# A third place for half of each group in the gradients of w1 and w2, and one buffer fewer for an output row

## The chip, the core and the metric

The kernel runs on one core of one Trainium2 chip. The metric is the time of one execution on the device, in microseconds (us). The core has five engines with their own instruction queues: TensorE (PE, matrix products, with weight loads shown apart as PEld), VectorE (DVE), ScalarE (ACT), GpSimd (POOL) and SyncE (SP). In this kernel SP issues the loads and POOL the stores; each queue is worked off in order.

## The reference

A gated mix of a spectral filter (a two-dimensional FFT, a product with a complex filter, the inverse) and a dense layer with squared ReLU, with its gradients by all inputs but B_x. What matters here is the dense layer and the gradients of its two weights:

```python
def _B_ref(x, w1, b1, w2, b2):          # x: 1 x 2048 x 1024, w1: 1024 x 3584, w2: 3584 x 1024
    h = jnp.einsum("bsd,df->bsf", x, w1) + b1
    zero = jnp.zeros_like(h)
    r = jnp.where(h > zero, h, zero)
    h = r * r
    out = jnp.einsum("bsf,fd->bsd", h, w2) + b2
    return out
# ...
g = _sigmoid((x * gate_w).sum(-1, keepdims=True))
return g * a + (1 - g) * b              # a: the spectral part, b: the dense part
# reference(): this output, and its vjp with grad_out
```

With db = (1 - g) * grad_out and dh = (db w2^T) * 2 r, the gradients are h^T db for w2 (3584 x 1024) and x^T dh for w1 (1024 x 3584). Both sum over the 2048 rows.

## The kernel before

Three stages follow each other on PE: a first one computes h2 = r * r and dh and stores both, turned, in DRAM (`h2T_scr`, `dhT_scr`); the second, `mlp_grads`, computes the two weight gradients; the third computes the dense output. Pieces of the FFT path are woven between their matrix products. In the profile the second stage lies from about 465 to 846 us.

The second stage goes through 14 groups of 512 columns: 7 of h2 (gradient of w2), then 7 of dh (gradient of w1). A group is loaded with four transposing DMAs into one of two tiles, `even` and `odd`:

```python
jobs = [(h2T_scr, fg) for fg in range(FG)] + [(dhT_scr, fg) for fg in range(FG)]
KH, FH = NT // 2, FGW // 2              # 8 row tiles, 256 columns
grp = {
    n: later["odd" if n % 2 else "even"][:].rearrange("p (t f) -> p t f", t=NT) for n in range(len(jobs))
}

def fetch(n, *halves):                  # column halves 0 and 1 of group n, each in two row halves
    if n < len(jobs):
        scr, fg = jobs[n]
        v_ = scr[:].rearrange("c p s -> (c p) s")[fg * FGW : (fg + 1) * FGW, :]
        for i in halves:
            f_ = slice(i * FH, (i + 1) * FH)
            for k in range(2):
                in_ = v_[f_, k * KH * P : (k + 1) * KH * P]
                after(turned(grp[n][:, k * KH : (k + 1) * KH, f_], in_), later["blocks"])
    elif n == len(jobs) and 1 in halves:
        later["block"] = blocks(h2T_scr)(0)
```

Each product is made of 2 x 2 quarters by Strassen's scheme in Winograd's form: seven chains of products, p1 to p7, in place of eight, with sums of quarters made on DVE beforehand. `a11`, `a12` are the two row halves of the first column half of a group, `a21`, `a22` those of the second; the sum S1 = a21 + a22 is written in place of a21.

```python
def left(g, *which, tie=None):
    (a11, a12), (a21, a22) = quads(grp[g], FH)
    # ... S3 = a11 - a21, S1 = a21 + a22 (in place), S2 = S1 - a11, S4 = a12 - S2

class Block:                            # 128 rows of either column half; two blocks to a group
    def __init__(self, k):
        self.g, self.part = divmod(k, 2)
        self.lo = wb.tile([P, D], BF16, name="wlo", tag="wlo", bufs=3)[:]
        self.hi = wb.tile([P, D], BF16, name="whi", tag="whi", bufs=2)[:]
        self.operands()

    def add(self, t_, h, kept):         # DVE; its line is 924 in the profile
        return V(out=self.side(t_, h), in0=self.flat(self.V[:]), in1=self.flat(kept[:]), op=ALU.add)

    def p1(self):
        self.X = mps.tile([P, H], FP32, name="pX", tag="pX", bufs=2)
        self.chain(self.X, self.a11, self.b11, True)
        self.c1 = self.kept("c1", 2)    # ACT copies pX
    def p2(self):
        self.V = mps.tile([P, H], FP32, name="pV", tag="pV", bufs=2)
        self.chain(self.V, self.a12, self.b21, True)
        self.first = self.add(self.lo, 0, self.c1)      # first half of the low rows
    def p5(self):
        self.chain(self.V, self.S[1], self.T[1], True)  # begins pV anew
    # ... p6, p7 on pX; p4 completes and stores self.hi
    def p3(self):
        self.chain(self.V, self.S[4], self.b22, False)
        self.ended = self.add(self.lo, 1, self.u2)      # second half of the low rows
        self.store(self.lo, 0)                          # POOL stores 256 KB
```

The class `Turned`, for the gradient of w1, does the same with x as the left operand and the group as the right one (products on line 987, sums of a group on line 1035; for w2 lines 913 and 887).

The order of the work in the steady state, the same in both halves of the stage:

```python
for k in range(2, NB // 2):
    a = blk.pop(k - 1)
    g, second = divmod(k, 2)
    b = blk[k] = Block(k)
    b.p1()
    b.p2()
    if second:
        fetch(g + 2, 0)
    a.p4()
    if not second:
        fetch(g + 1, 1)
    b.p6()
    a.p3()
    if second and g + 1 < FG:
        left(g + 1, 3, 1, tie=a.ended)
    # ...
    b.p5()
    b.p7()
    # ... left(g, 4), or left(g + 1, 2)
```

(`yield`s, at which pieces of the FFT path are put in, are cut.) At the passage from the seventh to the eighth group two blocks b and c of the gradient of w1 begin together: b.p1, b.p2, a.p4, a.p3, c.p1, c.p2, sum X3 of x, b.p5, b.p6, c.p5, c.p6, sum X4, b.p7, c.p7, b.p4, b.p3.

Of the kernel before, what the change touches and what calls it, by code (L numbers as in the profile page):

```python
# [10 lines left out]
P = 128  # L11
BF16 = mybir.dt.bfloat16
# [128 lines left out]
def kernel(  # L141
# [27 lines left out]
    S, D = xf.shape  # L169
    F = B_w1.shape[1]  # L170
    g = Geo(S, D, F)
    S2, DC, FC = g.S2, g.DC, g.FC
    R1, R2 = g.R1, g.R2
    NT = S // P
    Q, H, LW, W1 = D // 4, D // 2, g.Df + 1, g.Df
    FGW, FG, FGC = g.FGW, g.FG, g.FGC
# [4 lines left out]
    turned = lambda out, in_: nc.sync.dma_start(out=out, in_=in_, transpose=True)  # L181
# [12 lines left out]
    def pool(name, side="left", space=SBUF, stack=None, bufs=1):  # L194
        stack = ExitStack() if stack is None else stack
        kw = {} if space == DRAM else dict(side=side, reuse_waits="tile")
        return stack.enter_context(tc.tile_pool(name=name, bufs=bufs, space=space, **kw)), stack

    pers, _ = pool("pers", stack=ctx)
    dram, _ = pool("dram", space=DRAM, stack=ctx)  # L200
# [13 lines left out]
    h2T_scr = dram.tile([FC, P, S], BF16, name="h2T_scr")  # L214
# [19 lines left out]
    def after(ins, earlier, wait=mybir.DependencyClass.Sync):  # L234

        if earlier is not None:
            info = mybir.DependencyInfo(wait, mybir.DependencyReason.DATA)
            tc.add_manual_dep(ins.ins, earlier.ins.name, info, reason="paced")
# [386 lines left out]
    later = {}  # L625
# [183 lines left out]
    def mlp_grads():  # L809
        wb, wbs = pool("m2")  # L810
# [6 lines left out]
        def more_of_x(n, last):  # L817
            for t in range(len(loaded), min(len(loaded) + n, NT)):
                after(ld(out=xr[:, t, :], in_=x_perm[t]), last)
                loaded.append(t)  # L820

        jobs = [(h2T_scr, fg) for fg in range(FG)] + [(dhT_scr, fg) for fg in range(FG)]
        KH, FH = NT // 2, FGW // 2
        grp = {
            n: later["odd" if n % 2 else "even"][:].rearrange("p (t f) -> p t f", t=NT) for n in range(len(jobs))
        }

        def fetch(n, *halves):
            if n < len(jobs):
# [3 lines that stand above are left out]
                    f_ = slice(i * FH, (i + 1) * FH)  # L833
                    for k in range(2):
                        in_ = v_[f_, k * KH * P : (k + 1) * KH * P]
                        after(turned(grp[n][:, k * KH : (k + 1) * KH, f_], in_), later["blocks"])
            elif n == len(jobs) and 1 in halves:
                later["block"] = blocks(h2T_scr)(0)

        fetch(0, 0, 1)  # L840

# [13 lines left out]
        quads = lambda t_, w_: [[t_[:, j * KH : (j + 1) * KH, i * w_ : (i + 1) * w_] for j in range(2)] for i in range(2)]  # L855
# [15 lines left out]
            yield  # L871

        def left(g, *which, tie=None):
            (a11, a12), (a21, a22) = quads(grp[g], FH)
            made = S_.setdefault(g, {})
            for n in which:
                if n == 1:
                    made[1] = fp16(a21)
                else:
                    made[n] = sb.tile([P, KH, FH], FP16, name=f"S{n}", tag=f"S{n}", bufs=2 if n == 3 else 1)[:]  # L880
                x, y, op = {
                    3: lambda: (a11, a21, ALU.subtract),
                    1: lambda: (a21, a22, ALU.add),
                    2: lambda: (made[1], a11, ALU.subtract),
                    4: lambda: (a12, made[2], ALU.subtract),
                }[n]()
                later["sum"] = V(out=made[n], in0=x, in1=y, op=op)  # L887
                after(later["sum"], tie, mybir.DependencyClass.NoSync)

        class Block:  # L890

            def __init__(self, k):
                self.g, self.part = divmod(k, 2)
                self.lo = wb.tile([P, D], BF16, name="wlo", tag="wlo", bufs=3)[:]
                self.hi = wb.tile([P, D], BF16, name="whi", tag="whi", bufs=2)[:]
                self.operands()

            def operands(self):
                (a11, a12), (_, a22) = quads(grp[self.g], FH)
                self.A = {"11": a11, "12": a12, "22": a22, **S_.setdefault(self.g, {})}  # L900
                self.S, self.T = S_[self.g], T_
                self.a11, self.a12, self.a22 = a11, a12, a22
                self.b11, self.b21, self.b22 = b11, b21, b22
# [57 lines left out]
        class Turned(Block):  # L961

            def operands(self):
                (self.a11, self.a12), (_, self.a22) = quads(xr, H)
                (self.b11, self.b21), (_, self.b22) = quads(grp[self.g], FH)
                self.S, self.T = X_, T_[self.g]

            flat = staticmethod(lambda ap: ap.rearrange("p (j f) -> p j f", j=2))
# [49 lines left out]
                X_["last"] = made  # L1018

        def sums_of_group(g, *which, tie=None):  # L1020
            (g11, g21), (g12, g22) = quads(grp[g], FH)
            made = T_.setdefault(g, {})
            for n in which:
                if n == 3:
                    made[3] = fp16(g12)
                else:
                    tag = {1: "S3", 2: "S2", 4: "S4"}[n]
                    made[n] = sb.tile([P, KH, FH], FP16, name=f"G{n}", tag=tag, bufs=2 if n == 1 else 1)[:]
                x, y = {
                    1: lambda: (g12, g11),  # L1030
                    2: lambda: (g22, made[1]),
                    3: lambda: (g22, g12),
                    4: lambda: (g21, made[2]),
                }[n]()
                after(V(out=made[n], in0=x, in1=y, op=ALU.subtract), tie, mybir.DependencyClass.NoSync)  # L1035
# [23 lines left out]
        yield each  # L1059
        blk[1].p5()  # L1060
        left(0, 4)
        fetch(2, 0)
        yield each
        blk[1].p6()
        next(sums)
# [11 lines left out]
# [5 lines that stand above are left out]
            yield each  # L1082
# [3 lines that stand above are left out]
            yield each  # L1086
            a.p4()
            if not second:
                fetch(g + 1, 1)
            yield each  # L1090
            b.p6()
            yield each
# [3 lines that stand above are left out]
            if k >= 4:  # L1096
                more_of_x(2, a.last)
            yield each
            b.p5()
            if k == NB // 2 - 2:  # L1100
                sums_of_x(1, tie=a.ended)
            if k == NB // 2 - 1:
                sums_of_x(2, tie=a.ended)
            yield each
            b.p7()
            if not second:
                left(g, 4, tie=b.added)
            elif g + 1 < FG:
                left(g + 1, 2, tie=b.added)
            else:  # L1110
                sums_of_group(FG, 1, 2, tie=b.added)
            yield each
# [11 lines left out]
        flat = db_p.tile([P, NT * D], BF16, name="w2L", tag="dbn")  # L1124
        later["w2L"] = flat[:, 0 : FC * H].rearrange("p (c e) -> p c e", e=H)
        later["spare"] = flat[:, FC * H :]
        fetch(FG + 1, 1)
        yield each
        c.p1()
        yield each  # L1130
# [24 lines left out]
        for k in range(NB // 2 + 2, NB):  # L1155
            g, second = divmod(k, 2)
            b = Turned(k)
            b.p1()
            yield each
# [3 lines that stand above are left out]
            yield each  # L1163
            a.p4()
            if not second:
                sums_of_group(g, 3, 4)
            yield each
            b.p6()
            yield each
            a.p3()  # L1170
            if not second:
                fetch(g + 1, 1)
            yield each
            b.p5()
            yield each
            b.p7()
            if second and g + 1 < len(jobs):
                sums_of_group(g + 1, 1, 2, tie=b.added)
            yield each
            n = k - NB // 2 - 2  # L1180
            if n < FC // 4:
                rows_of_w2(later["w2L"], 4 * n, 0, b.added)
            a = b
# [11 lines left out]
    def blocks(scr):  # L1195
        v_ = scr[:].rearrange("c p s -> p c s")

        def one(k, earlier=None):
            t_ = later["odd" if k % 2 else "even"][:, 0 : FC * BW].rearrange("p (c b) -> p c b", b=BW)
            for h in range(2):  # L1200
                c_ = slice(h * FC // 2, (h + 1) * FC // 2)
                after(ld(out=t_[:, c_, :], in_=v_[:, c_, k * BW : (k + 1) * BW]), earlier)
            return t_

        return one
# [460 lines left out]
    for k in range(NT // 4):  # L1666
        i = 4 * k
# [129 lines left out]
```

## Time and profile before

| what | value |
|---|---|
| time, median of 3 runs | 1215.94 us (1215.14 to 1216.46) |
| span of the profiled run | 1213.8 us |
| TensorE clock granted | 0.999 of full speed |
| DMA moved | 234.44 MB, 193 GB/s on average |
| transposing loads from `h2T_scr` and `dhT_scr` | 56, four to a group |
| stores of `wlo`, of `whi` | 28 of 256 KB each, on POOL's queue |

How to read it: "busy" is the time in which an engine works on an instruction; waiting, branching and issuing of DMAs are not counted. A wait is put down to what released it last. "To landing" is the time from the issue of a DMA to its completion. In a table of stretches each row gives start and end, length, busy time of PE, PEld, DVE, ACT and POOL with the count of instructions, the granted clock, the busy share of the DMA engines and GB/s. `even` and `odd` hold the groups, `pX` and `pV` are the accumulators, `wlo` and `whi` the low and high output rows of a block, `S` and `G` sums of a group's quarters, `X` sums of x. Matrix products are pipelined, and their ends in the trace are modelled.

### The profile page before, as it was taken

Reading aid. Unit: us, or ns where it says so; the run is one execution under the profiler, and the core shown is the slowest. Engines: PE = TensorE matmul, PEld = TensorE weight load, DVE = VectorE, ACT = ScalarE, POOL = GpSimd, SP = SyncE. Lnnn points to the kernel's source line nnn. Section 1 sums busy time; section 2 is a strip of 40 time slices with the busy share of each in tenths; the row PEclk is TensorE's granted clock in tenths of the full one; section 3 lists DMA queues with packets and bytes.
Section 4 is the critical chain, followed back from the end, with each engine's and each line's share of the span. In section 5 each row is a group of like instructions: output and inputs, shape, how many; then the busy total and the mean of one; then the engine's idle time right before and its main releaser. Section 6 shows DMA issues by size and latency. Waiting matters only on the chain. (4 is left out here: it accounts for less than half of the span.)

```text
span 1213.8 us, 20077 instructions
## 1 busy us (share of the span) xinstructions
PE 1189.0 (98%) x7229; PEld 653.8 (54%) x7328; DVE 827.5 (68%) x1808; ACT 620.7 (51%) x1128; POOL 361.0 (30%) x587
## 2 busy tenths in 40 slices
PE   9999999999999999999999999999999999999997
PEld 5555555544444444444447889888444444444443
DVE  3546466586788977887789556665389756966464
ACT  4658767736777773444445245554455422332322
POOL 0124424413455542333333434444131000000000
PEclk9999999999999999999999999999999999999999
DMA  9668566486758598998998799956875699965550
GB/s 278 214 173 191 165 170 215 132 168 194 203 178 209 178 242 138 213 221 201 238 207 163 163 250 216 212 170 180 269 217 173 193 212 221 247 198 174 160 148 35
DMA packets 332383, 234.44 MB, mean 193 GB/s; under 512 B 197773, under 2 KB 291115, under 8 KB 332283
## 3 DMA queue, kind: packets, MB, share of 16 engines
q1 hardware_dynamic: 301856, 142.50, 52.2%
q0 software_dynamic: 30224, 90.61, 24.0%
q8 instruction: 57, 0.93, 0.3%
q14 instruction: 44, 0.35, 0.1%
q10 hardware_dynamic: 202, 0.04, 0.0%
HBM read 107.24 MB, written 81.81 MB: 156 GB/s over the span
## 5 line engine op out<-in xcount | busy, mean ns | idle before, releaser
L725 PE MATMUL ph<-xT,w1g 128*128 128x512 bf16 x866 | 214.6, 379 | 3.0 <-DMA w1g<-in_B_w_dram 1.2
L733 PE MATMUL pd<-dbT,w2T 128*128 128x512 bf16 x874 | 210.0, 379 | 1.0
L733 PEld LDWEIGHTS <-w2T 128*128 128x128 bf16 x896 | 87.1, 98 | 101.8
L737 DVE SCALAR_TENSOR_TENSOR dhT<-pd,rT 128x512 bf16<-128x512 f32 x112 | 76.8, 686 | 87.9 <-PE pd L733 76.1
L725 PEld LDWEIGHTS <-w1g 128*128 128x128 bf16 x896 | 85.2, 98 | 93.3 <-DMA w1g<-in_B_w_dram 1.5
L726 ACT ACTIVATE rT<-ph,b1col 128x512 bf16<-128x512 f32 x112 | 77.3, 690 | 67.3 <-PE ph L725 60.4
L987 PEld LDWEIGHTS <-res 128*128 128x128 bf16 (+1 forms) x896 | 86.7, 98 | 12.2 <-issue 2.0
L1339 PEld LDWEIGHTS <-dS 128*128 128x128 f16 x574 | 55.9, 98 | 66.3
L226 POOL DMA_DIRECT2D z_scr<-u x96 | 58.6, 616 | 105.5 <-ACT u L294 51.0
L226 POOL DMA_DIRECT2D r<-y_scr x96 | 58.3, 612 | 104.7 <-issue 44.4
L419 ACT CAST x<-px 64x512 f16<-64x512 f32 x128 | 74.1, 579 | 18.0 <-PE px L416 16.9
L727 ACT ACTIVATE h2T<-rT 128x512 bf16<-128x512 bf16 x112 | 70.6, 630 | 2.1
L987 PEld LDWEIGHTS <-X 128*128 128x128 f16 x672 | 64.7, 98 | 8.0
L1339 PEld LDWEIGHTS <-odd 128*128 128x128 bf16 (+1 forms) x392 | 38.2, 98 | 47.7 <-issue 2.1
L1339 PEld LDWEIGHTS <-even 128*128 128x128 bf16 (+1 forms) x392 | 38.1, 98 | 44.6
L913 PEld LDWEIGHTS <-S 128*128 128x128 f16 x336 | 32.9, 98 | 39.7 <-DVE S L887 0.3
L456 POOL DMA_DIRECT2D y_scr<-pc x64 | 36.3, 567 | 52.7 <-DVE pc L453 43.6
L1360 DVE TENSOR_TENSOR cu<-pV,u 128x512 f16<-128x512 f32 x28 | 19.3, 689 | 44.0 <-PE pV L1339 38.2
L779 POOL DMA_DIRECT2D h2T_scr<-h2T x28 | 20.7, 738 | 95.7 <-ACT h2T L727 95.5
L568 ACT CAST rt<-pki 128x1024 f16<-128x1024 f32 x32 | 32.4, 1013 | 29.2 <-PE pki L566 29.2
L1312 POOL DMA_DIRECT2D out_dram<-gxo x14 | 7.6, 540 | 131.8 <-DVE gxo L1311 131.8
L426 DVE TENSOR_TENSOR tt<-x,w 128x1028 f16<-128x1028 f16 (+1 forms) x32 | 22.2, 693 | 33.8 <-ACT x L420 20.8
(265 smaller groups left out, 2472.8 us busy)
## 6 DMA issues: line engine op xcount, KB each, us to landing
h2T_scr<-h2T POOLq DMA_DIRECT2D x28, 512.0 KB, 4.2
dhT_scr<-dhT POOLq DMA_DIRECT2D x28, 512.0 KB, 5.1
z<-z_scr SPq DMA_DIRECT2D x64, 128.0 KB, 3.3
y_scr<-pc POOLq DMA_DIRECT2D x64, 128.0 KB, 3.8
ax_scr<-yo POOLq DMA_DIRECT2D x32, 256.0 KB, 4.2
w1g<-in_B_w_dram SPq DMA_DIRECT2D x14, 512.0 KB, 4.9
out_dram<-whi POOLq DMA_DIRECT2D x28, 256.0 KB, 4.6
out_dram<-wlo POOLq DMA_DIRECT2D x28, 256.0 KB, 5.3
```

The costliest lines, as they stand in the source:

```text
L226: issue(out=a, in_=b) if stored else issue(out=b, in_=a)
L419: nc.scalar.copy(out=x[lanes[n], c, :, 0:HW], in_=px[lanes[c], n])
L456: st(out=y_scr[:][c, :, :, h].rearrange("r x t l -> (r x) t l"), in_=pc[:, n])
L568: nc.scalar.copy(out=rt[n][:], in_=pk[:])
L725: mm(ph[:], lhsT=w1g[:, dc, fc % 2 * P : (fc % 2 + 1) * P], rhs=xT[:, dc, ss], start=(dc == 0), stop=(dc == DC - 1))
L726: nc.scalar.activation(rT[:], ph[:], ACT.Relu, bias=b1col[:, fc : fc + 1])
L727: nc.scalar.activation(h2T, rT[:], ACT.Square)
L733: mm(pd[:], lhsT=w_[:, ec, fc % FGC * P : (fc % FGC + 1) * P], rhs=dbT[:, ec, ss], start=(ec == 0), stop=(ec == DC - 1),)
L737: return STT(out=dhT, in0=pd[:], scalar=2.0, in1=rT[:], op0=ALU.mult, op1=ALU.mult, accum_out=gb1part[:, fc, sb : sb + 1],)
L913: self.mm = mm(acc[:], lhsT=lhs[:, t, c_], rhs=rhs[:, t, :], start=start and t == 0, stop=t == KH - 1, skip_group_check=True,)
L987: ins = mm(acc[:, j * FH : (j + 1) * FH], lhsT=lhs[:, t, c_], rhs=rhs[:, t, :], start=start and first_ is None, stop=t == KH - 1, skip_gro ...
L1339: pe(mm(acc[:], lhsT=lhs[:, c, :], rhs=rhs[:, c, :], start=start and c == 0, stop=c == KH - 1, skip_group_check=True,))
```

## The change

The first column half of a group keeps its place in `even` or `odd`. For the second column half there are now three places used in turn: the second halves of `even` and `odd`, and a new tile `third` of 128 x 16 x 256. So the second half of a group can be loaded a whole group earlier, while that of the group before is still in use: `fetch(g + 1, 1)` becomes `fetch(g + 2, 1)`, and group 2 is loaded whole at the start. The new tile takes 8 KB in each partition; one of three `wlo` buffers (2 KB each) is given up. The change is meant to let loads run further ahead of their use.

```diff
-        grp = {
-            n: later["odd" if n % 2 else "even"][:].rearrange("p (t f) -> p t f", t=NT) for n in range(len(jobs))
-        }
+        spare_half = wb.tile([P, NT, FH], BF16, name="third", tag="third")[:]
+        both_of = [later[which][:].rearrange("p (t f) -> p t f", t=NT) for which in ("even", "odd")]
+        lasts = [both_of[0][:, :, FH:], spare_half, both_of[1][:, :, FH:]]
+        grp = {n: (both_of[n % 2][:, :, 0:FH], lasts[n % 3]) for n in range(len(jobs))}
+        halves_of = lambda g: [[h_[:, j * KH : (j + 1) * KH, :] for j in range(2)] for h_ in grp[g]]
 ... fetch():
-                        after(turned(grp[n][:, k * KH : (k + 1) * KH, f_], in_), later["blocks"])
-            elif n == len(jobs) and 1 in halves:
-                later["block"] = blocks(h2T_scr)(0)
+                        after(turned(grp[n][i][:, k * KH : (k + 1) * KH, :], in_), later["blocks"])
 ... left(), operands(), sums_of_group(): quads(grp[g], FH) becomes halves_of(g)
 ... Block.__init__():
-                self.lo = wb.tile([P, D], BF16, name="wlo", tag="wlo", bufs=3)[:]
+                self.lo = wb.tile([P, D], BF16, name="wlo", tag="wlo", bufs=2)[:]
 ... ahead of the loop:
-        fetch(2, 0)
+        fetch(2, 0, 1)
 ... in the loop, after a.p4():
             if not second:
-                fetch(g + 1, 1)
+                fetch(g + 2, 1)
 ... at the passage to w1, after a.p3():
-        fetch(FG + 1, 1)
+        fetch(FG + 2, 1)
 ... in the loop of w1, after a.p3():
             if not second:
-                fetch(g + 1, 1)
+                fetch(g + 2, 1)
+                if g + 1 == len(jobs):
+                    later["block"] = blocks(h2T_scr)(0)
```

More of the change, by code (lines that the diff above doesn't have):

```diff
@@ L873, in left @@
         def left(g, *which, tie=None):
-            (a11, a12), (a21, a22) = quads(grp[g], FH)
+            (a11, a12), (a21, a22) = halves_of(g)
             made = S_.setdefault(g, {})
@@ L898, in operands @@
             def operands(self):
-                (a11, a12), (_, a22) = quads(grp[self.g], FH)
+                (a11, a12), (_, a22) = halves_of(self.g)
                 self.A = {"11": a11, "12": a12, "22": a22, **S_.setdefault(self.g, {})}
@@ L964, in operands @@
                 (self.a11, self.a12), (_, self.a22) = quads(xr, H)
-                (self.b11, self.b21), (_, self.b22) = quads(grp[self.g], FH)
+                (self.b11, self.b21), (_, self.b22) = halves_of(self.g)
                 self.S, self.T = X_, T_[self.g]
@@ L1020, in sums_of_group @@
         def sums_of_group(g, *which, tie=None):
-            (g11, g21), (g12, g22) = quads(grp[g], FH)
+            (g11, g21), (g12, g22) = halves_of(g)
             made = T_.setdefault(g, {})
```

## The prediction

> **What bounds the kernel now.** I read the page's busy times first, then the table of stretches, then the waits of PE inside the stretch that computes the two weight gradients (about 460 to 850 us), and last, instruction by instruction, the queue of DVE and the loads there.
>
> ```profile
> PE 1189.0 (98%) x7229; PEld 653.8 (54%) x7328; DVE 827.5 (68%) x1808; ACT 620.7 (51%) x1128; POOL 361.0 (30%) x587
> ...
> 460.00:850.00 390.00, 384.32 (x2782) 259.81 (x2796) 282.90 (x609) 183.25 (x340) 156.84 (x253) 1.00 0.91 200
> ```
>
> PE is busy for 384.3 of 390 us in the stretch that the change touches. At most 5.7 us can be won there, 0.5% of the whole. What PE waited for in that stretch, longest first:
>
> ```profile
> PE pV L987 <- DVE wlo L924: 1.5, 1, 1.5
> PE pki L566 <- DVE rf L558: 1.4, 5, 0.4
> PE pki L566 <- DVE rf L559: 0.9, 2, 0.4
> PE pb L848 <- DVE gb1b L846: 0.7, 1, 0.7
> PE pX L987 <- ACT u L972: 0.2, 1, 0.2
> ```
>
> The list is complete, and no load of a group (`even`, `odd`) stands in it. The longest wait is for an addition into `wlo`, the low output rows. So the stage hangs on PE, with DVE close behind at one place, and DMA is not what PE waits for. The DMA engines are crowded all the same (share 0.91, the last column but one of the stretch).
>
> [...] whether two `wlo` are too few is worked out below. [...]
>
> ```profile
> L949 POOL DMA_DIRECT2D out_dram<-wlo x14: 540/545/617, 489.3 to 651.7; - x14
> ...
> DMA to landing us min/median/max: 2.3/5.3/9.9
> ```
>
> (Two lines of the answer for the tile `wlo`.) [...]
>
> **The change, part by part.** *Instructions.* The built program has the same PE, ACT and POOL instructions in the same order; DVE has one `wlo` addition moved back by two places; all 56 transposing loads are kept. No busy time is added or removed. Only waits can change.
>
> *The loads.* The second column half of group g-1 comes free after p4 of its last block, in both kernels at the same place of the program. Before, it is then filled with group g+1; after, with group g+2. In the steady state the transfers therefore start at the same moments, only their content is one group later. What the readers gain is slack, so I looked at the slack they had. The last load of group 2 is issued at 496.50 and lands 4.8 us later at 501.3; the first sum on that group starts at 511.86, so it was there 10.6 us early. For group 8 it is 647.80 + 6.0 = 653.8 against 667.32, 13.5 us early. Groups 3 to 13, taken in the same way, have about 10 us or more. A wait that isn't there can't be removed: 0 us gained.
>
> At the start of the stage group 2 is now loaded whole, two transposing loads more ahead of the FFT's next `z` load on SP's queue:
>
> ```profile
> 463.73 13.38 SPq L181 DMA_TRANSPOSE odd<-h2T_scr  x4
> 477.21 0.53 SPq L378 DMA_DIRECT2D ab<-c_ab  x1
> 477.83 14.98 SPq L181 DMA_TRANSPOSE even<-h2T_scr  x3
> 492.91 1.01 SPq L388 DMA_DIRECT2D z<-z_scr  x2
> ```
>
> Seven issues took 28.4 us, 4.1 each, so `z` goes out 8 us later, at 501, and lands (4.2 us in the trace) at 505. Its reader starts at 506.6: nothing, or a microsecond of DVE.
>
> *The low rows.* A block takes a `wlo` at p2 (first addition), completes it at p3 in the next block's round, and stores it. With three buffers the first addition of block k+2 never met the store of block k; with two it must wait for that store's landing. I took the start of each first addition of before and the landing (issue time plus its time to landing) of the store of two blocks earlier. Of 26 pairs, 8 come late (block: addition wanted / store landed): 2: 492.5/496.3; 9: 581.8/584.6; 10: 594.3/597.4; 11: 607.2/609.5; 12: 622.0/623.9; 15: 654.3/661.7; 17: 686.6/688.8; 18: 700.0/703.1. That is 3.8, 2.8, 3.1, 2.3, 1.9, 7.4, 2.2 and 3.0 us in which DVE stands still, since its queue is in order.
>
> PE feels this only when the p5 chain of that block, which overwrites the same `pV` bank, is due: addition start + 0.69 us against the start of p5. The room is 4.1, 4.7, 5.1, 5.1, 2.9, 2.2, 4.3 and 4.1 us. Taken singly only block 15 overruns. Two things make it more than that:
>
> 1. Blocks 9 to 12 follow each other. A late addition makes the queue behind it late, with it the completing addition, its store, and the addition two blocks on, less the idle time of DVE between. Carrying that on (idle time 0.5, 1.5 and 3.9 us between a first addition and the next completing one) gives lateness of 2.8, 5.5, 6.2 and 4.2 us; with room 4.7, 5.1, 5.1, 2.9 PE is pushed back by 0.4, then to 1.1, then to 1.3 us. Sum 1.3.
> 2. At block 15, the passage from the gradient of w2 to that of w1, DVE has no idle time:
>
> ```profile
> 653.97 0.41 DVE L409 TENSOR_TENSOR pm<-z 128x512 f16<-128x512 f16 x1
> 654.30 0.68 DVE L924 TENSOR_TENSOR wlo<-pV,c 128x512 bf16<-128x512 f32 x1
> 654.90 2.28 DVE L1015 TENSOR_TENSOR X<-res,X 128x4096 f16<-128x4096 bf16 x1
> ...
> 671.98 0.68 DVE L924 TENSOR_TENSOR wlo<-pV,u 128x512 bf16<-128x512 f32 x1
> ```
>
> (start, duration, engine, line, output <- inputs). The chain of PE and the store that matter there, the latter from the DMA view of 651 to 652 us:
>
> ```profile
> 657.18 1.91 PE L987 MATMUL pV<-G,res 128*128 128x256 f16 x16
> ...
> out_dram<-wlo POOLq DMA_DIRECT2D x1, 256.0 KB, 9.9
> ```
>
> The p5 due at 657.18 would start at about 662.4 (5.2 us lost), and the addition of 671.98, for which PE already waits 1.5 us, moves by the rest of 7.4: 2.2 more. Sum 7.4 if that store again takes 9.9 us; with the median 5.3 it is 2.8. I take 5, since the broadcast of b2 and of the gate, 512 KB, still stands ahead of it on POOL's queue.
>
> Block 2 has its 3.8 us of lateness in 4.1 of room, and two more loads beside its store; I put 0.7 there, and 0.5 for blocks 17 and 18, which start with a DVE behind by some microseconds. Sum: 1.3 + 5 + 0.7 + 0.5 = 7.5. PE has no idle time later to win it back. Off this I take 1 us, because a stalled PE also delays what makes the next addition wanted: 6.5, so 1215.9 + 6.5 = 1222.4.
>
> **Rivals.**
> 1. *The landing times shift.* [...] if the earlier start of group 2 spreads the traffic, [...] no addition waits: 1215 us. For it: the nine stores that landed in 2.3 to 3.6 us left 2.6 to 5.6 us until the buffer would be wanted, one of them 0. Against it: after the start, transfers begin at the same moments as before.
> 2. *Prefetch pays.* The loads' slack hides a wait that the profile puts down to others, such as the 1.5 us or the DVE waits marked issue: 1213 us. Against it: the 10 us found above.
> 3. *The waits lock together.* The chain of addition, completion, store, addition becomes the pace of the blocks, near 15 us a block against 12.5 to 14.7 in the crowded part: 1 to 2 us for each of some ten blocks, 1232 us. For it: the carried lateness above grows over three blocks. Against it: later blocks have 1 to 5 us of slack each.
>
> **Range and chances.** The middle is 1222; rivals 1 and 2 set the low end at 1214, rival 3 the high end at 1231. 2% is 24 us: it can't be gained (5.7 us are idle in the stage), and could be lost only well past rival 3. Faster 0.01, same 0.96, slower 0.03.
>
> **What would show it.** Right: first additions into `wlo` in the after profile with idle time ended by the store's DMA, on DVE, largest near 655 us; PE's wait for `wlo` or `pV` there up from 1.5 to some 5 to 8 us; the idle time of PE in the stage up by about the loss; no change ahead of 460 us; the loads' landing 20 us or more ahead of their first sum, and nothing gained from it. Wrong: no DMA-ended wait on DVE at L924 (stores land sooner), PE waits unchanged with the time up or down elsewhere, or group sums that start earlier than before.

## The result and the profile after

| what | before | after |
|---|---|---|
| time, median of 4 runs | 1215.75 us | 1233.80 us (1230.93 to 1235.08) |
| ratio, 95% interval | | 1.0145 (1.0126 to 1.0164) |
| span of the profiled run | 1213.8 us | 1233.3 us |
| TensorE clock granted, mean | 0.999 | 0.992 |

The change costs 18 us, where the prediction had 6.5, in a range up to 1231. Below, medians are of all runs of a kernel; ratios leave out its slow runs, so where the two differ, the ratio counts.

The page's busy times, then the stretch of the two weight gradients, from the table of stretches (start and end, length, busy time of PE, PEld, DVE, ACT and POOL, granted clock, share of the DMA engines, GB/s):

```profile
PE 1201.3 (97%) x7328; PEld 656.3 (53%) x7328; DVE 827.3 (67%) x1808; ACT 621.3 (50%) x1128; POOL 360.8 (29%) x587
```

```profile
460.00:850.00 390.00, 374.00 (x2634) 247.91 (x2632) 273.00 (x574) 175.37 (x325) 147.46 (x238) 0.98 0.88 192
460.00:869.00 409.00, 392.85 (x2799) 262.73 (x2797) 282.86 (x609) 183.37 (x340) 156.94 (x254) 0.98 0.87 190
```

The stretch that took 390 us takes 409. DVE, ACT and POOL do the same work in it (282.86 us of DVE against 282.90). PE sits idle for 16.2 us in place of 5.7, and its granted clock is 0.98: part of its busy time was work at a granted clock of 0.50, called half clock below, which the prediction had nowhere. What PE waited for, complete:

```profile
PE pV L987 <- DVE wlo L924: 6.2, 2, 4.8
PE pki L566 <- DVE rf L558: 5.2, 5, 4.0
PE pX L913 <- DVE S L887: 2.2, 1, 2.2
PE pV L913 <- DVE wlo L924: 1.2, 2, 0.7
PE pki L566 <- DVE rf L559: 0.9, 2, 0.4
PE pX L987 <- ACT u L972: 0.2, 1, 0.2
```

(us in total, times, longest.) Three waits are long. Only the first, 4.8 us on block 15's `wlo`, was predicted. The second is for `rf`, a small addition of the FFT path; the third for sums at the start of the stage. Behind them stand waits of DVE on DMA:

```profile
DVE wlo L924 <- DMA out_dram<-wlo: 25.7, 7, 7.0
DVE T L864 <- DMA h2T_scr<-h2T: 2.4, 1, 2.4
```

Before, neither stood in the list. The first is the predicted one: 7 additions waited 25.7 us for a store of low rows (predicted: 8, and 26.5 us). An eighth, block 9's, stands in the list under another name (4.6 us, `ACT gw`), but it too started 0.12 us after its store had landed, as six of the seven did. The second is new: sum T2 of db's quarters waits for a store of h2, which belongs to the stage before. From the view of the tile `wlo`, the stores themselves:

```profile
DMA to landing us min/median/max: 2.3/4.9/9.5
```

They land as before (2.3/5.3/9.9). The passage, first DVE, then PE:

```profile
659.06 0.42 DVE L409 TENSOR_TENSOR pm<-z 128x512 f16<-128x512 f16 x1
666.45 0.69 DVE L924 TENSOR_TENSOR wlo<-pV,c 128x512 bf16<-128x512 f32 x1 [6.97 <-DMA out_dram<-wlo]
667.05 2.28 DVE L1015 TENSOR_TENSOR X<-res,X 128x4096 f16<-128x4096 bf16 x1
```

```profile
667.19 3.57 PE L987 MATMUL pV<-G,res 128*128 128x256 f16 x16 [4.75 <-DVE wlo L924]
670.56 2.47 PE L987 MATMUL pX<-G,X 128*128 128x256 f16 x16
672.86 1.36 PE L987 MATMUL pX<-third,X 128*128 128x256 f16 x11
```

The 16 products of p5 take 3.57 us after the wait; before, 1.91. The end of the passage, the addition that stood at 671.98 us before, and the products that wait for it:

```profile
684.12 0.68 DVE L924 TENSOR_TENSOR wlo<-pV,u 128x512 bf16<-128x512 f32 x1
```

```profile
684.86 1.91 PE L987 MATMUL pV<-even,res 128*128 128x256 bf16 x16 [1.48 <-DVE wlo L924]
```

From the first of these additions to the second DVE takes 17.7 us in both kernels (654.30 to 671.98, 666.45 to 684.12), and PE waits 1.5 us for the second in both. So through the passage PE follows DVE: it loses the 7.0 us by which DVE is late, first 4.9 in the wait, then 2.1 at half clock. That at full clock the 2.1 us would have been waits further on is shown below, by the broadcasts. Block 18, where the prediction had almost nothing, looks so on DVE and on PE:

```profile
711.05 1.22 DVE L1035 TENSOR_TENSOR even<-even 128x2048 f16<-128x2048 bf16 x1
715.92 0.69 DVE L924 TENSOR_TENSOR wlo<-pV,c 128x512 bf16<-128x512 f32 x1 [3.65 <-DMA out_dram<-wlo]
716.53 0.28 DVE L558 TENSOR_TENSOR rf<-r 128x256 f16<-128x256 f16 x1
716.73 0.28 DVE L559 TENSOR_TENSOR rf<-r 128x256 f16<-128x256 f16 x1
```

```profile
712.47 0.39 PE L566 MATMUL pki<-ki,re 128*128 128x128 f16 x4
716.87 0.70 PE L566 MATMUL pki<-ki,rf 128*128 128x128 f16 x4 [4.01 <-DVE rf L558]
```

The addition that waits belongs to block 18, but PE doesn't need it yet. It needs `rf`, 0.28 us of work, which stands right behind the addition in DVE's queue.

The order of PE's instructions is the same in both kernels, so the 7328 weight loads can be set side by side one by one. How far the kernel after lies behind, at the steps of this curve (from the two traces; the column "before" is the time in the kernel before):

| before, us | step | seen there |
|---|---|---|
| 474 to 476 | +4.0 | PE waits 2.2 us for a sum `S`, DVE for h2's store; then half clock, 1.6 of the 4.0 |
| 489 | -0.7 | a wait of the kernel before (for `gb1b`) is gone |
| 592 to 613 | +1.8 | PE waits for additions into `wlo` at blocks 10 and 11 |
| 657 | +4.9 | PE waits for `wlo` of block 15 |
| 657 to 662 | +2.1 | half clock |
| 701 | +3.8 | PE waits for `rf` behind `wlo` of block 18 |
| 701 to 706 | +2.8 | half clock |
| 872, 918 | +0.8 | loads of w2 and `rf` in the third stage |

At the last load it is 19.5, the difference of the two spans. About 13 us are waits and 6.5 half clock. Not all of the latter is a cost of its own: in the passage it took the place of waits, and 0.7 us are won back at 489 us. At block 18 it is one: behind that wait it is DVE that waits for PE, 5.6 us at 723.75. The table of stretches, cut at the moments where the clock changes, shows the half clock (the last column but two is the clock):

```profile
473.71:477.12 3.41, 1.21 (x6) 0.36 (x4) 3.41 (x3) 3.22 (x6) 0.00 (x0) 1.00 1.19 307
477.12:480.54 3.42, 3.41 (x9) 1.22 (x10) 3.42 (x3) 0.00 (x0) 2.12 (x4) 0.50 1.09 169
...
661.44:664.86 3.42, 1.00 (x10) 0.75 (x8) 0.00 (x0) 1.60 (x3) 1.07 (x2) 1.00 1.25 153
664.86:668.27 3.41, 1.08 (x6) 0.75 (x6) 1.82 (x2) 0.00 (x0) 0.00 (x0) 0.50 1.05 216
668.27:671.68 3.41, 3.41 (x18) 2.35 (x17) 3.41 (x6) 0.00 (x0) 0.82 (x2) 0.50 0.00 0
671.68:675.10 3.42, 3.42 (x31) 2.88 (x30) 3.39 (x5) 0.88 (x2) 3.32 (x5) 1.00 0.43 120
...
712.64:716.06 3.42, 0.22 (x4) 0.04 (x1) 0.14 (x1) 0.59 (x1) 0.00 (x0) 1.00 1.03 305
716.06:722.88 6.82, 6.01 (x30) 4.33 (x31) 2.08 (x4) 2.21 (x4) 2.56 (x4) 0.50 0.59 178
```

Each of the three long waits falls in a stretch of 3.41 us in which PE is busy for 0.35, 0.29 and 0.06 of it, and the next stretch has clock 0.50. In the kernel before the clock was 0.50 only at the very end, from 1212.1 us.

### The profile page after: what moved, and what is told of

Same layout as the page of the kernel before. It is cut to its first block, busy times and chain, and to the rows that moved or that the text cites. A ratio compares the mean times of both kernels' runs of the same rounds, so it can differ in the third digit from the quotient of the medians.

```text
span 1233.3 us, 20172 instructions
## 1 busy us (share of the span) xinstructions
PE 1201.3 (97%) x7328; PEld 656.3 (53%) x7328; DVE 827.3 (67%) x1808; ACT 621.3 (50%) x1128; POOL 360.8 (29%) x587
## 5 line engine op out<-in xcount | busy, mean ns | idle before, releaser
L725 PE MATMUL ph<-xT,w1g 128*128 128x512 bf16 x896 | 218.6, 379 | 1.2 <-DMA w1g<-in_B_w_dram 1.2
L1341 PE MATMUL pX<-wT,dS 128*128 128x512 f16 x196 | 44.7, 379 | 0.0
```

What stands on the lines that cost most here:

```text
L725: mm(ph[:], lhsT=w1g[:, dc, fc % 2 * P : (fc % 2 + 1) * P], rhs=xT[:, dc, ss], start=(dc == 0), stop=(dc == DC - 1))
L1341: pe(mm(acc[:], lhsT=lhs[:, c, :], rhs=rhs[:, c, :], start=start and c == 0, stop=c == KH - 1, skip_group_check=True,))
```

## The experiments

The theory after this reading: four causes in a sum. (a) Low rows in two buffers wait for stores. (b) A DVE instruction that waits holds back the FFT's `rf`. (c) Half clock comes from PE's waits: it followed those of 2.2, 4.8 and 4.0 us. (d) The new tile shifts other buffers, and T2's now lies over a buffer of h2. The rival in each case is that loads one group ahead, or the traffic they make, are at the root. The addresses in a partition, from the built programs:

```
           before            after             third place last
third                        100288-108480     160128-168320
wlo        100288-106432     108480-112576     100288-104384
T2         135552-143744     141696-149888     133504-141696
h2T (1st)  147392-151488     147392-151488     147392-151488
```

**Two buffers alone** (kernel before).

```diff
-                self.lo = wb.tile([P, D], BF16, name="wlo", tag="wlo", bufs=3)[:]
+                self.lo = wb.tile([P, D], BF16, name="wlo", tag="wlo", bufs=2)[:]
```

> The kernel before with two wlo buffers and nothing else. Theory (the second buffer's wait for its store, plus a half clock of PE after each wait over 2 us): DVE waits for the store's landing of some 25 us in sum, PE 5 us late at the passage to w1 and 4 us at the first FFT pieces of w1 (about 700 us), each followed by some 6.8 us at half clock; no wait at the start of the stage: 1215.8 + 14 = 1230 us. Rival A (the new load order is the cause): 1216 us. Rival B (the wait alone, the clock is another matter): 1225 us.

Measured 1231.57 us, ratio 1.0123 (1.0106 to 1.0139), against 1216.17 for before on that chip. Its waits, of PE and then of DVE on DMA:

```profile
PE pV L987 <- DVE wlo L924: 7.8, 2, 5.6
PE pki L566 <- DVE rf L558: 7.3, 5, 6.1
```

```profile
DVE wlo L924 <- DMA out_dram<-wlo: 23.3, 5, 7.8
```

The waits at 657 and 701 us are here without the third place and without other loads, and half clock follows both (mean clock of the profiled run 0.995, 0.992 in the kernel after); the wait on h2's store isn't here. So (a) makes most of the loss, and the loads have no part in it.

**The addresses alone** (kernel before, with 6 KB that nothing uses).

```diff
+        pad = wb.tile([P, 3 * D], BF16, name="pad", tag="pad")
```

> The kernel before with 6 KB more in each partition ahead of the sums' buffers (an unused tile), all instructions and their order as before. Theory (T2's place now covers a buffer from which the last h2T is still being stored): T2 waits 2.4 us for that store at 471 us, PE waits 2.2 us for S2, then runs 3.4 us at half clock: 4 us more, 1220 us. Rival (the wait at 471 us in the profile after comes from the loads of group 2 that run earlier): 1216 us.

Measured 1223.0 us over 11 runs, ratio 1.0033 (1.0002 to 1.0064), which is 4 us; the trace lies 3.8 behind at the end. In the waits of DVE and in the stretches:

```profile
DVE T L865 <- DMA h2T_scr<-h2T: 3.6, 1, 3.6
```

```profile
474.79:478.20 3.41, 0.29 (x2) 0.18 (x3) 3.41 (x3) 1.70 (x3) 1.38 (x3) 1.00 1.13 246
478.20:481.61 3.41, 3.41 (x10) 1.23 (x9) 3.41 (x3) 0.32 (x1) 0.74 (x2) 0.50 1.39 238
```

A tile that nothing reads or writes brings the wait and the half clock. That is (d), shown.

**The third place with three buffers** (kernel after; to make room, three small tiles of the sum of b1 lie in a tile that is no longer used).

```diff
-                self.lo = wb.tile([P, D], BF16, name="wlo", tag="wlo", bufs=2)[:]
+                self.lo = wb.tile([P, D], BF16, name="wlo", tag="wlo", bufs=3)[:]
-            gb1 = wb.tile([P, FC], FP32, name="gb1", tag="gb1")
+            gb1 = kf_[:, 0 : 2 * FC].bitcast(FP32)        # gb1b and gb1r likewise
```

> The changed kernel with three wlo buffers again (the three small tiles for the gradient of b1 lie in a constant no longer used, to make room). Theory: no wait for a wlo store is left, only the one at 471 us from the shifted place (2.2 us and the half clock after it): 1215.8 + 4 = 1220 us. Rival (the loads ahead gain something that the lost buffer hid): 1216 us or less. Rival (they cost something through the DMA engines): 1224 us or more.

Measured 1221.09 us over 20 runs, ratio 1.0045 (1.0023 to 1.0068). No wait on a store of low rows is left in the trace; the wait on h2's store is (2.3 us), with half clock (mean 0.998), and the trace ends 2.6 us behind. So the loads ahead gain nothing that these runs show, and the rest is (d).

**Low rows in halves, each stored when ready** (kernel after: two tiles of half the width with 2 buffers each, the same memory as two whole ones).

```diff
-                self.lo = wb.tile([P, D], BF16, name="wlo", tag="wlo", bufs=2)[:]
+                self.lo = [wb.tile([P, H], BF16, name=f"wlo{h}", tag=f"wlo{h}", bufs=2)[:] for h in range(2)]
... p2, p3: each addition writes its own half, and the store of that half follows at once
```

> The changed kernel, in which the two halves of the low rows lie in tiles of their own, two buffers each (the same 4 KB), and each half is stored as soon as it is added, so the store of a first half is issued a whole block earlier. Theory: first additions find their buffer free, the waits for wlo stores fall from 25.7 us to about 0, and the time to 1215.8 + 4 = 1220 us (the wait at 471 us stays). Rival (28 more stores crowd POOL's queue and the DMA engines): waits for y_scr and r grow, 1226 us or more.

Measured 1218.3 us over 20 runs, ratio 1.0006 (0.9987 to 1.0025). No addition waits for a store: the first half goes out at p2, not at p3. T2 still waits, and PE with it for 2.4 us, yet without half clock (mean 1.0), cut at the same kind of moments:

```profile
471.41:474.82 3.41, 2.80 (x13) 1.08 (x11) 1.75 (x1) 2.67 (x5) 0.00 (x0) 1.00 1.11 232
474.82:478.23 3.41, 1.67 (x8) 0.79 (x9) 3.41 (x4) 1.44 (x3) 1.65 (x4) 1.00 1.22 269
478.23:481.65 3.42, 3.42 (x18) 1.56 (x16) 3.42 (x3) 0.58 (x1) 1.03 (x2) 1.00 1.08 180
```

The wait lies across two stretches, and PE is busy for 2.80 us of the one and 1.67 us of the other (0.49 of it). By 500 us, the trace has lost 2.6 us, against 3.3 in the kernel after.

**The FFT's `rf` ahead of the waiting addition** (kernel with two buffers alone). DVE's order changes in one place: the two `rf` come ahead of block 18's addition; two copies of ACT and one load on POOL's queue move with them.

```diff
-        for _ in range(LEAD):
-            yield
-        folded(0)
+        for n in range(LEAD):
+            if n == LEAD - 2:
+                folded(0)
+            yield
```

> The kernel before with two buffers for low output rows, and the first folded tile of the rows brought back (the two VectorE additions rf and their ScalarE copies) put two turns earlier, so that VectorE has them ahead of block 18's addition that waits for a store. If the 6.1 us wait of TensorE at the start of that work, and the half clock after it, come from the additions rf standing behind the waiting addition in VectorE's order: that wait goes, no half clock follows it, and the time is 7 to 9 us below that of two buffers alone (1231.6), so 1223 to 1225. Rival: block 18's addition itself is what TensorE's next p5 has to wait for, so the wait only moves to the second half of that block: then 1229 to 1232. The wait of block 15 near 657 us stays about 5 to 6 us in both.

Measured 1224.02 us, ratio 1.0056 (1.0032 to 1.0079): 7.5 us less. PE's waits:

```profile
PE pV L988 <- DVE wlo L925: 6.2, 2, 5.1
PE pki L566 <- DVE rf L558: 1.2, 4, 0.4
```

The 6.1 us are gone, the mean clock is 0.996 in place of 0.995, and block 15's wait stays. Block 18's addition still starts after 4.4 us in which DVE is idle, and PE's lag grows by 0.1 us there: the addition itself had the room, the `rf` behind it had not. That shows (b).

**The broadcasts of b2 and of the gate later** (kernel with two buffers alone).

```diff
-        st(out=b2_bc, in_=B_b2.partition_broadcast(P))
-        st(out=gatew_bc, in_=gate_w.partition_broadcast(P))
+        after(st(out=b2_bc, in_=B_b2.partition_broadcast(P)), later["tie"])
+        after(st(out=gatew_bc, in_=gate_w.partition_broadcast(P)), later["tie"])
```

> The kernel before with two buffers for low output rows, and the two broadcasts of b2 and of the gate's weights (512 KB on the queue of the stores, issued just ahead of block 13's store) issued some time later. If block 13's low rows land late (9.9 us) because those broadcasts go ahead of them: the store lands in about 5 us, block 15's addition waits some 2.5 us in place of 7.8, TensorE's wait near 657 us falls from 5.6 us to under 1, and the time is 5 to 7 us below that of two buffers alone (1231.6), so 1225 to 1227. Rival: the landing is late because the engines are filled by the transposed loads and other traffic of the passage: then nothing changes, 1230 to 1232.

Measured 1232.08 us, ratio 1.0103 (1.0044 to 1.0161): the time missed the expectation, while the mechanism held in part. Block 13's store lands in 6.4 us in place of 10.4, block 15's addition waits 3.9 in place of 7.8, PE at p5 1.7 in place of 5.6, without half clock there. PE then waits again, at two places of the passage, and has lost 4.0 us at its end, as much as the addition waited. With two buffers alone it lost 7.9 us for 7.8, with 3.4 us at half clock. So at the passage half clock is no cause of its own: PE loses what DVE loses, with it or without. But the broadcasts now go out at 855 us, ahead of the loads of w2 for the third stage. There PE waits 4.5 us in place of at most 0.6, half clock follows at 889 (mean over the profiled run 0.996), and the trace falls back by 4.7 us more. So the 512 KB ahead of it made up some 4 of the store's 10.4 us; the rest was not taken apart.

**T2 computed twice, and three times** (kernel before).

```diff
             V(out=T_[2], in0=b22, in1=T_[1], op=ALU.subtract)
+            V(out=T_[2], in0=b22, in1=T_[1], op=ALU.subtract)     # a third one for "thrice"
```

> The kernel before with the VectorE sum T2 of the first block computed twice (the same subtraction again, same result): about 2.2 us more of VectorE on the path to TensorE's first matmuls that need it, no buffer changed. If a wait of TensorE of about 2 us starts half clock there: the cost is the wait plus about 1.7 us, so 2.2 to 4 us in all, and the profile shows 3.41 us at clock 0.50 right behind it. If the half clock of the shifted layout had to do with memory or transfers and not with the wait: no half clock, cost 2.2 us or less, 1216.5 to 1218.4.

> The kernel before with the VectorE sum T2 of the first block computed three times: about 4.4 us more of VectorE on the path to TensorE's first matmuls that need it, no buffer changed. If waits of TensorE start half clock: a wait of some 4 us and 3.4 to 6.8 us at clock 0.50 behind it, in all 5.5 to 8 us, 1221.5 to 1224. If half clock does not follow from the wait: 4.4 us at most, 1220.5.

Twice: 1220.09 us, ratio 1.0022 (0.9995 to 1.005). PE waits 2.0 us with no half clock there (the eight products behind it take 1.90 us, those ahead of it 1.89), and 1.8 more for a `wlo` at 496 us. Thrice: 1221.06 us, ratio 1.0031 (1.0002 to 1.0061). The scheduler put one chain of PE elsewhere, so that PE waited 2.6 us and not 4.4; 3.41 us of half clock follow (the eight products at 479.35 us take 2.45 us, those at 482.28 1.89). As a ruler the pair is poor: the added 2.3 us each didn't reach PE as planned, and the profile of "thrice" has an unrelated wait of 8 us at 760 us. What it does show is half clock after a wait that only VectorE's arithmetic makes, with no buffer moved, which speaks for (c), while the pair's other wait, 2.0 us, had no half clock behind it.

**The third place allocated last** (kernel after: T2's buffer no longer lies over h2T's; no engine's computation changes its order, but at the start of the stage some loads change places on SP's queue).

```diff
-        spare_half = wb.tile([P, NT, FH], BF16, name="third", tag="third")[:]
+        sb, sbs = pool("m2s")
+        tb, tbs = pool("m2t")
+        spare_half = tb.tile([P, NT, FH], BF16, name="third", tag="third")[:]
... further down, where `m2s` was opened before:
-        sb, sbs = pool("m2s")
```

> The changed kernel, with the third place allocated behind the buffers of the sums in place of ahead of everything, so that T2's buffer (133504 to 141696) no longer lies over the first stage's h2T buffer (147392 to 151488). No order of any engine's work changes. If the wait at 471 us and the half clock behind it come from the shift of addresses alone: VectorE's 2.4 us wait for the store of h2T and TensorE's 2.2 us wait for the sums are gone, no half clock near 477 us, and the time falls by 2.5 to 4 us from that of the changed kernel (1233.8), to 1230 to 1231.5. Rival: the two-buffer waits and the transposed loads are the whole loss: no change, 1233 to 1235. The third place now lies over buffers of dhT (160128 to 168320), but its first load has over 10 us of room.

Measured 1230.01 us, ratio 1.0123 (1.011 to 1.0136): 3.8 us less, though from four runs each, and the two ratios' intervals overlap. The trace is clearer: no wait on h2's store, no half clock near 477 us (mean 0.995, 0.992 in the kernel after), and nothing lost by 500 us, where the kernel after has lost 3.3. That is (d) again, from the other side. Later the two traces differ in other ways too: DVE waits 8.9 us for block 15's buffer in place of 7.0, and PE 2.0 us for `rf` in place of 4.0.

**The same with `rf` early.**

> The changed kernel with the third place allocated last and also the first folded tile of the rows brought back put two turns earlier. If the causes add up: the wait at 471 us (2.5 to 4 us) and the one at 701 us with its half clock (7 to 7.5 us) are both gone, and what is left is block 15's wait near 657 us with its half clock (about 6.5 us) and a us of small ones: 1222.5 to 1224.5. If the causes lock together (a later start only moves a wait on): 1227 to 1231.

Measured 1224.85 us, ratio 1.0098 (1.007 to 1.0125): 5.2 us less again, 0.35 above the expected range. The causes add only roughly: moving `rf` gave 7.5 us in the kernel with two buffers, where the wait for it was 6.1 us and not 2.0. In its trace the lag grows from 1.1 to 9.2 us at the passage, and DVE waits 8.0 us for block 15's buffer: that and the carried lateness ahead of it are what is left.

**Two sums late** (kernel before). The last steps look for a version better than both.

```diff
-        sums_of_group(FG + 1, 1, 2, tie=c.added)
         yield each
         b.p4()
         yield each
         b.p3()
+        sums_of_group(FG + 1, 1, 2, tie=b.ended)
```

> The kernel before, with the sums G1 and G2 of the second group of the gradient of w1 (two VectorE subtractions of 1.22 us, 667.3 and 669.1 us, in its passage from one gradient to the other) put behind block 14's last addition. They stand ahead of that block's addition wlo in VectorE's order, for which TensorE waits 1.5 us at 671 us. If VectorE's order is what TensorE waits for: the wait goes and the time falls by 1 to 2 us, to 1214 to 1215.5. Rival: the sums are needed by block 16 soon after, the wait moves to TensorE's matmuls with G: 1215.5 to 1217.

Measured 1215.38 us over 22 runs against 1215.13, ratio 1.002 (0.9997 to 1.0043). PE's wait falls from 1.5 to 0.8 us and the trace ends 1.4 us earlier, but the timed runs don't show it as a gain.

**All of it** (kernel after, low rows in halves, third place last, two sums late).

> The changed kernel with its low rows stored in two halves as soon as each is ready (2 buffers of each half), the third place allocated last, and the sums G1, G2 late as above. If the three causes named are all there is: no wait on a store of low rows, none at 471 us, no half clock, and the loads one group ahead give nothing: the time of the kernel before, less the 1 to 2 us of the late sums, 1213.5 to 1216. If the third place itself costs something apart from its address (more loads under way at once): 1217 to 1219.

Measured 1215.58 us over 13 runs, ratio 1.001 (0.9996 to 1.0023): level with before. It has a new wait of its own. The third place now lies over buffers of dhT, its two loads are issued at 475.8 and 478.4 us (468.8 and 476.0 in the kernel after), and a sum waits for them:

```profile
488.35 1.22 DVE L888 TENSOR_TENSOR S<-odd,third 128x2048 f16<-128x2048 bf16 x1 [1.30 <-DMA third<-h2T_scr]
```

PE waits 2.1 us for a cast behind it, with half clock at 491 us. That the new place is why the loads go out late isn't shown: SP's wait for a store of dhT is only 0.5 us, and a load of `odd` now goes out ahead of them. No version here is shown to beat the kernel before.

## Why the prediction was wrong

**Right.** *The loads ahead: 0 us.* Three low-row buffers beside the third place leave only the shift of addresses. *Late additions*: 8 predicted, and 7 or, with block 9's, 8 found; block 3 was late in place of 12. *Blocks 9 to 12*: 1.3 predicted, 1.8 in the curve. *Block 15, the path*: lateness less room at p5, and the rest at the end of the passage. The working had 5.2 and 2.2 us; found were 4.9 in the wait and 2.1 at half clock. *More loads at the start*: `z` went out at 497.9, not at 501, and no engine shows a wait for it. Rivals 1 and 2 fell, since stores land as late as before and prefetch pays nothing. Rival 3 has the right size, 1232, for the wrong reason: the lateness came mostly in three places, not from block to block.

**Wrong, four terms.**

1. *"PE feels this only when the p5 chain of that block, which overwrites the same `pV` bank, is due."* This is the step that failed most. DVE works its queue off in order (at block 18 `rf` ran at 716.53, right behind the addition that had waited 3.65 us), so the room of a late addition is that of everything behind it. For block 18 I had 3.0 us of lateness in 4.1 of room, and 0.5 us for blocks 17 and 18 together. The `rf` behind it had next to no room: PE waits 4.0 us. Taken with the half clock it is 6.6 us in the curve, and 7.5 when `rf` is moved in the kernel with two buffers.
2. *"I take 5"* at block 15, between 7.4 for a store that takes 9.9 us and 2.8 for the median. The store took 9.5 us, and the loss was 7.0. That 5 is near the 4.9 us of the wait is luck.
3. *A wait costs its own length.* The sum had no term for the clock. At block 18 half clock adds 2.8 us. At the start it adds 1.6, of which 0.7 are won back; at block 15 nothing that DVE's lateness would not have cost. So it is under 4 of the 19.5 us. In the kernel after it followed PE's waits of 2.2, 4.8 and 4.0 us, for 3.42, 6.82 and 6.82 us.
4. *"Only waits can change"*, and then only those of the buffers in the diff. The new tile moved the buffers allocated behind it by 6 KB (8 for the third place, less 2), and T2's came over one that a store of the stage before was still reading. Cost 3.3 us in the curve, 3.8 to 4 in the timed runs, and absent from the prediction. The addresses were to be had from the built program.

In the curve, block 15 is 7.0 us, block 18 6.6, the start 3.3, blocks 10 and 11 1.8, and the third stage 0.8, of which the prediction had nothing: 19.5 in this pair of profiled runs, while the medians differ by 18.05. The predicted 6.5 were 5, 0.5, 0.7 (for block 2, which cost PE nothing), 1.3 and 0, less 1 us that the curve doesn't show as a term of its own.

## What to carry to other kernels

When a buffer is given up, list for every instruction that may now wait what stands behind it in its engine's queue, and take the least room of all of those. Compare the addresses of the buffers too, above all at the seam of two stages: here T2 waited 2.4 us for a store of the stage before. Price a long wait of PE at its length and, beside it, with half clock behind it. At block 18 that was 3.8 us in the curve and 2.8 more; at block 15 the 2.1 us of half clock cost nothing of their own, since DVE held PE back through the same stretch anyway. Low rows stored in halves kept the memory of two buffers and had no waits on stores at all.

## What the runs showed that I had not expected

In the kernel after, PE's clock falls to 0.50 at 477.12, 664.86 and 716.06 us, moments 55 and 15 times 3.413 us apart, and in the 3.41 us ahead of each PE was busy for 0.35, 0.29 and 0.06 of the time. I had taken the length of a wait to decide. But low rows in halves have a wait of 2.4 us that lies across two stretches, with busy shares of 0.82 and 0.49 (rows above), and the clock stays at 1.00. With all of it together, a wait of 2.1 us lies in one stretch, with a share of 0.40, and half clock follows:

```profile
488.04:491.46 3.42, 1.36 (x7) 0.59 (x7) 2.79 (x4) 0.56 (x1) 0.55 (x1) 1.00 1.27 255
491.46:494.87 3.41, 3.41 (x10) 1.22 (x8) 3.41 (x9) 0.43 (x2) 0.57 (x1) 0.50 1.16 261
```

So of these two it was the shorter wait that half clock followed; a rule for other kernels is not shown.
